# Constants loaded in three parts instead of one, with the first order table laid anew

## The chip, the cores and the metric

The kernel runs on one core of a Trainium2 chip. The metric is the device time of one execution in microseconds (us), as the median of the runs. The core has a matrix engine (TensorE, PE in the profile, with its weight loads as PEld), a vector engine (DVE), a scalar engine (ACT), GpSimd (POOL) and SyncE (SP), which here only issues loads and stores.

## What is computed

The reference is an attention-like retention layer without softmax, followed by a gated layer that mixes along the sequence:

```python
B, H, S, D = 8, 8, 576, 64
scores = (q @ k.T) / sqrt(D)                       # per batch and head
ret    = scores * where(rel >= 0, gamma[h] ** rel, 0)
x      = (ret @ v)                                 # -> (B, 576, 512)
h      = relu(x @ w_in)                            # (B, 576, 1024)
u, v   = h[..., :512], h[..., 512:]
v_n    = (v - mean(v)) / sqrt(var(v) + 1e-6)
v_s    = einsum('ts,bsd->btd', w_spatial, v_n) + b_spatial[None, :, None]
out    = (u * v_s) @ w_out
```

## The kernel before

The retention is computed in chunks of 128 rows (four per batch, and a tail of 64). A chunk `c` of batch `b` goes through these steps, and the order tables name each by a letter:

- `d.b.c`: its loads: `qk` (q and k, 512 KB), `kn` (k by rows, 256 KB), `vv` (v, 256 KB); chunks 2 and 3 of batch 0 come as one load of 1024 KB into the room of `u` and of `lent_wout`.
- `g.b.c`: PE makes the scores (`r<-qk`), then DVE multiplies them with the decay mask (`at<-r,fixed_terms`).
- `k.b.c`: `kn` is multiplied with powers of gamma. `q.b.c`: q is multiplied with powers of gamma into `qsc`.
- `p.b.c`: PE makes the update of the state (`r<-vv,kn`), then the state is taken on: `sh` (after half the chunk), `dec`, `st`.
- `b.b.c`: PE adds what the state carries (`r<-qsc,sh` and `r<-qsc,st`) in two halves, with a two-element copy on ACT between them (`r<-warm`), then the values (`r<-at,vv`); the result is split into a rounded part and the rest (`slot`, on ACT, then DVE).

The gated layer follows as large matrix products. `w.kind.i` turns a quarter of a weight matrix, which comes as float64 words, into a rounded part and the rest: one step on DVE or POOL, one on ACT, two on DVE, one on ACT (`win<-lent_vn`), one on POOL or DVE. `D.kind.i` loads such a quarter (512 KB), `c.a` loads the constants, `c.t` a mask for the tails. `z.i.1` is one product of 512 columns on a tile of zeros (`m<-wsp`), whose result nobody reads; there are 43 of them. I call them idle products.

The order of all work is written out in tables of such names: `ORDER` for batches 0 and 1 and the beginning of 2, then `STEADY` once for each batch, then `LAST`. Each name, when its turn comes, runs the chain's next step, and each engine keeps the order in which its instructions were written. `BANKS` says which of four result banks of `m` each large product takes.

The constants are one array, with 780 numbers (3120 bytes) for each of 128 rows, 390 KB in all, and one load:

```python
fixed_terms = cp.tile([P, 2 * NP * D + NP * D + H + NP], F32, name="fixed_terms")
am = fixed_terms[:, :512]...       # the decay mask, used by g (DVE)
qs = fixed_terms[:, 512:768]...    # powers for q, used by q (POOL, DVE)
kd = fixed_terms[:, 768:768 + H]   # powers for k, used by k
sd = fixed_terms[:, 768 + H:]      # powers for the state, used by p
```

SP issues loads in the order of the table. Each load counts on one of eight semaphores in turn, so the ninth waits until the first has landed, and so on.

Of the kernel before, what the change touches and what calls it, by code (L numbers as in the profile page):

```python
# [18 lines left out]
P = 128  # L19
# [29 lines left out]
    w.1.2.pp b.0.1 p.0.1.aa w.1.2.pp b.0.1 b.0.1 z.20.1 v.0.0 z.27.1 z.17.1 z.39.1 z.22.1 w.1.1.vp b.0.1 p.0.1.aa
    b.0.1 v.0.1 w.1.2.pp w.1.2.pp k.0.2.a g.0.2 p.0.2.aa w.1.2.pp w.1.1.vp w.1.3.vp w.1.2.pp v.0.0 z.42.1 v.0.1  # L50
    z.36.1 v.0.0 v.0.0 v.0.1 v.0.1 D.0.2 D.0.1 d.0.3 w.0.2.pp q.0.2.p p.0.1.aa w.0.2.pp p.0.2.aa g.0.2 p.0.2.aa
    p.0.2.aa w.0.2.pp w.0.1.vp w.0.1.vp w.0.1.vp w.0.2.pp w.0.1.vp T.0 S d.1.0 S d.1.0 d.1.0 c.t D.0.0 S d.1.1
    d.1.1 d.1.1 t.0.p q.0.3.p k.1.0.p k.0.3.a b.0.2 g.0.3 b.0.2 v.0.0 t.0.p b.0.2 b.0.2 p.0.3.ap p.0.2.aa b.0.2
    v.0.0 b.0.2 p.0.3.ap v.0.1 v.0.0 v.0.0 t.0.p g.0.3 v.0.1 z.26.1 z.29.1 z.11.1 z.5.1 v.0.2 v.0.2 v.0.2 z.9.1
    v.0.2 z.23.1 z.24.1 z.14.1 v.0.0 p.0.3.ap p.0.3.ap w.0.0.vp b.0.3 s.2.p v.0.1 b.0.3 g.1.0 v.0.0 w.0.0.vp v.0.2
    g.1.0 w.0.0.vp b.0.3 b.0.3 p.1.0.pp g.1.1 e.0.v e.0.v e.0.v w.0.0.vp v.0.1 v.0.4 v.0.4 v.0.4 z.16.1 z.35.1
    s.1.p b.0.3 w.0.2.pp p.1.0.pp w.0.0.vp v.0.1 b.0.3 v.0.3 v.0.3 v.0.4 v.0.3 v.0.3 q.1.0.p s.2.p k.1.1.p s.1.p
    p.1.0.pp w.0.0.vp d.1.2 S S v.0.2 w.0.1.vp v.0.2 v.0.2 s.3.p v.0.2 v.0.4 v.0.1 v.0.2 U.0 U.1 b.1.0 v.0.4 s.5.p
    v.0.4 v.0.3 s.0.p p.1.0.pp v.0.4 p.1.1.pp v.0.4 b.1.0 U.1 v.0.3 U.0 v.0.3 s.4.p g.1.1 v.0.3 v.0.3 v.0.4 v.0.3
    v.0.4 b.1.0 b.1.0 D.2.1 d.1.2 T.1 D.2.0 D.2.2 d.1.2 s.3.p w.0.2.pp q.1.1.p d.1.3 d.1.3 d.1.3 D.0.3 s.0.p G.1.2  # L60
    q.1.2.p p.1.0.pp s.5.p s.4.p v.0.4 v.0.4 p.1.1.pp p.1.1.pp p.1.1.pp w.0.1.vp k.1.2.p p.1.1.pp w.0.3.pv V.0.0
    V.0.0 V.0.0 V.0.0 V.0.3 V.0.0 V.1.0 b.1.0 V.0.0 b.1.0 V.0.3 w.2.1.vp w.2.1.vp V.1.0 w.2.1.vp V.1.2 V.0.2
    w.2.1.vp w.2.0.vv V.1.2 w.2.0.vv b.1.1 p.1.2.pa w.2.1.vp b.1.1 w.0.3.pv w.2.0.vv G.1.2 w.2.0.vv w.0.3.pv
    w.0.3.pv g.1.2 b.1.1 b.1.1 w.0.3.pv V.0.2 V.1.1 G.0.2 v.1.0 D.2.3 d.2.0 d.2.0 A.0.5.v A.0.0.v w.0.3.pv g.1.2
    p.1.2.pa w.2.2.vv G.0.3 V.1.1 w.2.0.vv p.1.2.pa p.1.2.pa G.0.2 q.1.3.p A.0.1.p k.1.3.p w.2.2.vv G.0.3 A.0.2.v
    A.0.6.v t.1.p V.0.1 G.0.1 p.1.2.pa V.0.1 b.1.1 b.1.1 w.2.0.vv v.1.0 A.0.9.v A.0.12.v w.2.2.vv p.1.3.pp b.1.2
    b.1.2 A.0.3 A.0.7 A.0.13.v A.0.14 P.0.1.p w.2.2.vv G.0.1 g.1.3 t.1.p b.1.2 b.1.2 v.1.0 V.1.3 v.1.0 G.1.3 v.1.1
    v.1.1 v.1.1 v.1.1 A.0.15.v p.1.3.pp w.2.3.vp p.1.3.pp w.2.1.vp d.2.1 d.2.0 d.2.1 b.1.2 t.1.p g.1.3 b.1.2 V.1.3
    A.1.5.p v.1.0 w.2.3.vp G.1.3 w.2.3.vp w.2.3.vp p.1.3.pp k.2.0.v v.1.0 b.1.3 b.1.3 p.2.0.vp b.1.3 g.2.0 b.1.3
    G.1.1 e.1.v P.0.0.p v.1.0 e.1.v e.1.v v.1.0 G.1.1 P.0.0.p P.0.1.p v.1.4 v.1.4 v.1.4 y.1.2.0 v.1.4 p.2.0.vp  # L70
    v.1.1 v.1.1 w.2.3.vp v.1.0 v.1.1 v.1.0 b.1.3 w.2.2.vv y.1.2.0 v.1.4 A.0.10 P.1.0.v y.1.1.0 y.1.1.0 A.0.4.v
    A.1.1.v w.2.2.vv v.1.1 v.1.1 v.1.1 g.2.0 p.2.0.vp y.1.0.0 F.0.0.0 y.1.0.0 F.0.0.0 P.1.1.v A.0.11.v A.0.8.v
    P.1.1.v b.1.3 v.1.4 F.0.0.2 v.1.2 v.1.2 F.0.0.1 v.1.2 v.1.2 v.1.4 w.2.3.vp F.0.0.1 F.0.0.2 v.1.2 A.1.0.v
    p.2.0.vp p.2.0.vp A.1.2.p A.1.3 P.1.0.v F.0.1.0 F.0.0.0 F.0.0.1 A.1.6.v A.1.9.v v.1.2 A.1.12.p v.1.4 A.1.13.v
    A.1.7 F.0.1.0 F.0.1.1 v.1.2 F.0.1.1 F.0.0.3 F.0.0.3 v.1.4 v.1.4 v.1.4 v.1.4 v.1.2 v.1.4 q.2.0.v F.0.0.3 F.0.1.0
    F.0.1.1 F.0.0.2 F.0.1.3 F.0.1.3 A.1.14 v.1.3 v.1.3 v.1.3 v.1.3 F.0.1.2 g.2.1 b.2.0 v.1.3 v.1.3 v.1.3 F.0.1.2
    v.1.3 b.2.0 v.1.3 y.1.3.1 y.1.2.1 y.1.3.1 k.2.1.a y.1.2.1 y.1.1.1 A.2.1.v A.1.4.p A.2.5.v A.1.15.p A.2.0.p
    A.2.2.v A.2.6.v v.1.3 A.2.9.v A.1.8.v A.2.12.v y.1.1.1 A.2.7 v.1.2 b.2.0 b.2.0 T.2 d.2.1 p.2.1.vv d.2.2 d.2.2
    d.2.2 F.0.1.3 y.1.3.0 g.2.1 v.1.2 X.1.1.2 X.1.1.2 A.2.3 A.2.10 A.1.10 b.2.0 X.1.0.0 X.1.0.1 y.1.0.1 q.2.1.v
    t.2.v A.2.11.v p.2.1.vv y.1.3.0 A.2.8.v b.2.1 b.2.1 p.2.1.vv p.2.1.vv k.2.2.v p.2.1.vv A.1.11.v X.1.0.1 X.1.0.0  # L80
    A.2.13.v A.2.14 y.1.0.1 A.2.15.v g.2.2 b.2.1 p.2.2.vv b.2.1 d.2.3 d.2.3 d.2.3 X.1.1.3 X.1.1.0 X.1.1.1 g.2.2
    A.2.4.v p.2.2.vv X.1.1.3 p.2.2.vv p.2.2.vv X.1.1.0 b.2.1 Y.1.3.p Y.1.1.v k.2.3.v Y.1.1.v X.1.1.1 Z.1.5.vv
    X.1.0.2 q.2.2.p b.2.2 b.2.2 Y.1.3.p Z.1.7.vv p.2.2.vv X.1.0.2 Z.1.6.vv p.2.3.vp t.2.v b.2.2 g.2.3 b.2.2
# [967 lines left out]
```

## Time and profile before

| | |
|---|---|
| time, median of 3 runs (lowest to highest) | 503.83 us (503.58 to 503.89) |
| profiled execution, its own time | 504.22 us |
| its span, from first to last instruction | 502.4 us |
| PE busy | 495.2 us, 99% of the span |
| DVE, ACT, POOL busy | 391.3, 259.4, 154.1 us |

The profiled execution took 1.8 us more than its span, which is launch and end around it. It is 0.39 us above the median. Busy time is the time in which an engine had an instruction running; the ends of matrix products are modelled, so a wait of PE that is shorter than about the length of a product can hide in it. Times in the rows count from the start of the span.

### The profile page before, as it was taken

What the parts mean: (1) busy time and instruction counts of PE and PEld (TensorE: products, weight loads), DVE (VectorE), ACT (ScalarE), POOL (GpSimd) and SP (SyncE); (2) the same over time, 40 slices, a digit from 0 to 9 for tenths busy, and PEclk for the clock granted to TensorE, in tenths of its full rate; (3) what the DMA queues carried; (4) which work ended last, traced back from release to release, by engine and by line L of the source; (5) the groups of instructions that cost most, each with busy time, mean ns of one, the idle gap of its engine ahead of it and who ended that gap; (6) DMA issues with size and microseconds to landing.
All of it is one profiled execution on the core that took longest, in us unless ns stands there. A gap on an engine that the chain in (4) does not pass through costs nothing.

```text
span 502.4 us, 17010 instructions
## 1 busy us (share of the span) xinstructions
PE 495.2 (99%) x7335; PEld 472.8 (94%) x7335; DVE 391.3 (78%) x869; ACT 259.4 (52%) x587; POOL 154.1 (31%) x133
## 2 busy tenths in 40 slices
...
DMA packets 26429, 55.53 MB, mean 111 GB/s; under 512 B 2929, under 2 KB 11249, under 8 KB 26098
## 3 DMA queue, kind: packets, MB, share of 16 engines
...
q14 instruction: 18, 0.15, 0.1%
...
## 4 chain that ended last, share of the span: by engine, by line
PE 94%; DVE 2%; ACT 1%; DMA 1%; issue 1%; POOL 0%; SPq 0%; ACTq 0%
PE m L203 79%; PE r L203 14%; DMA vv<-in_qkv 1%; ACT places L203 0%; DVE x L203 0%; POOL x L203 0%; DVE u L203 0%; DVE lent_vn L203 0%; DVE m L203 0%; ACT slot L203 0%; SPq L203 0%; DVE o L203 0%; DVE xt L203 0%; ACT xt L203 0%; DVE places L203 0%
## 5 line engine op out<-in xcount | busy, mean ns | idle before, releaser
L203 PE MATMUL m<-wsp,vn 128*128 128x288 f32 x768 | 112.7, 296 | 0.0
L203 PEld LDWEIGHTS m<-wsp,vn 128*128 128x128 f32 x768 | 105.0, 188 | 0.6
L203 DVE TENSOR_TENSOR u<-m,u 128x288 f32<-128x288 f32 (+1 forms) x132 | 57.1, 438 | 23.2 <-PE m L203 11.9
L203 ACT COPY u<-m 128x288 f32<-128x288 f32 (+1 forms) x92 | 34.8, 386 | 40.8 <-PE m L203 33.4
L203 PE MATMUL m<-slot,win 128*128 128x288 f32 x336 | 49.8, 296 | 0.0
L203 PEld LDWEIGHTS m<-slot,win 128*128 128x128 f32 x336 | 46.3, 188 | 0.9 <-ACT vn L203 0.2
L203 ACT CAST slot<-u 128x576 fp32r<-128x576 f32 x32 | 21.5, 675 | 45.3 <-DVE u L203 44.6
L203 DVE SCALAR_TENSOR_TENSOR u<-u,m 128x288 f32<-128x288 f32 x48 | 21.3, 451 | 26.6 <-PE m L203 26.4
L203 PE MATMUL m<-slot,wout 128*128 128x288 f32 x264 | 37.5, 294 | 0.0
L203 PEld LDWEIGHTS m<-slot,wout 128*128 128x128 f32 x264 | 36.0, 188 | 0.2
L203 PE MATMUL m<-win,slot 128*128 128x512 f32 (+1 forms) x168 | 36.2, 349 | 0.0
L203 ACT CAST places<-u 128x576 fp32r<-128x576 f32 x21 | 14.2, 675 | 39.0 <-DVE u L203 39.0
L203 POOL TENSOR_TENSOR dec<-st,fixed_terms 128x256 f32<-128x256 f32 x16 | 14.3, 895 | 64.6 <-DVE st L203 64.6
L203 POOL TENSOR_TENSOR qk<-qk,fixed_terms 128x512 f32<-128x512 f32 (+1 forms) x16 | 21.9, 1369 | 35.3 <-PE r L203 29.9
L203 PEld LDWEIGHTS m<-win,slot 128*128 128x128 f32 x168 | 26.7, 188 | 4.2 <-DVE slot L203 0.5
L203 PE MATMUL m<-quarter,slot 128*128 128x256 f32 x216 | 28.9, 281 | 0.1
L203 POOL TENSOR_TENSOR slot<-u,slot 128x576 fp32r<-128x576 f32 x7 | 10.0, 1436 | 59.5 <-ACT slot L203 53.9
L203 PEld LDWEIGHTS m<-quarter,slot 128*128 128x128 f32 x216 | 27.1, 188 | 0.7 <-ACT u L203 0.3
L203 PE MATMUL m<-wtl,vt 128*128 128x288 f32 (+1 forms) x128 | 27.2, 295 | 0.0
L203 PE MATMUL m<-places,wout 128*128 128x288 f32 x168 | 26.3, 297 | 0.0
L203 PE MATMUL m<-slot,part 128*128 128x288 f32 x168 | 25.3, 298 | 0.0
L203 DVE TENSOR_TENSOR at<-r,fixed_terms 128x512 f32<-128x512 f32 x32 | 21.9, 683 | 3.9 <-PE r L203 2.0
...
## 6 DMA issues: line engine op xcount, KB each, us to landing
qk<-in_qkv SPq DMA_DIRECT2D x30, 512.0 KB, 4.0
kn<-in_qkv SPq DMA_DIRECT2D x30, 256.0 KB, 4.6
vv<-in_qkv SPq DMA_DIRECT2D x30, 256.0 KB, 4.3
...
lent_slot<-in_w_v SPq DMA_DIRECT2D x4, 512.0 KB, 8.4
raw<-in_w_u SPq DMA_DIRECT2D x4, 512.0 KB, 10.8
```

What stands on the lines that cost most here:

```text
L203: ins = op(*args, **kw)
```

## The change

The array of constants becomes three, each with its own tile and load: `steps` (powers for k and for the state, 12 numbers a row, 6 KB in all) into `fixed_steps`, `terms` (the mask, 512 numbers a row, 256 KB) into `fixed_terms`, and `qterms` (powers for q, 256 numbers a row, 128 KB) into `qs`. In the tables `c.k`, `c.a` and `c.q` load them. `ORDER` and `BANKS` are new; `STEADY` and `LAST` stay. Every engine has the same instructions as before, in kind, number and shape, in another order; two loads are added on SP. The number of idle products stays at 43.

```diff
-    d.0.0 m z.41.1 z.34.1 d.0.0 c.a d.0.0 k.0.0.v q.0.0.p z.33.1 z.37.1 z.1.1 z.12.1 z.18.1 z.25.1 z.15.1 z.10.1
+    d.0.0 z.37.1 z.38.1 c.k d.0.0 m z.25.1 z.22.1 z.8.1 z.41.1 z.14.1 z.39.1 z.3.1 k.0.0.v d.0.0 g.0.0 c.q D.1.0
+    c.a q.0.0.p D.1.3 d.0.1 d.0.1 d.0.1 p.0.0.va p.0.0.va z.32.1 z.10.1 z.17.1 w.1.0.vp z.1.1 z.13.1 z.12.1 b.0.0
...
-    fixed_terms = cp.tile([P, 2 * NP * D + NP * D + H + NP], F32, name="fixed_terms")
-    am = fixed_terms[:, :512].rearrange("r (i p n) -> r i p n", i=2, p=NP)
-    qs = fixed_terms[:, 512:768].rearrange("r (p n) -> r p n", p=NP)
-    kd = fixed_terms[:, 768:768 + H].rearrange("r (h n) -> r h n", n=1)
-    sd = fixed_terms[:, 768 + H:].rearrange("r (p n) -> r p n", n=1)
+    fixed_terms = cp.tile([P, 2 * NP * D], F32, name="fixed_terms")
+    am = fixed_terms.rearrange("r (i p n) -> r i p n", i=2, p=NP)
+    fixed_steps = cp.tile([P, H + NP], F32, name="fixed_steps")
+    kd = fixed_steps[:, :H].rearrange("r (h n) -> r h n", n=1)
+    sd = fixed_steps[:, H:].rearrange("r (p n) -> r p n", n=1)
+    qs = cp.tile([P, NP, D], F32, name="qs")
...
-        "c": lambda k: dma_one(*{"a": (fixed_terms, terms), "t": (amt, tmask)}[k]),
+        "c": lambda k: dma_one(*{"a": (fixed_terms, terms), "k": (fixed_steps, steps), "q": (qs, qterms), "t": (amt, tmask)}[k]),
...
-    terms = np.concatenate([a.reshape(P, -1) for a in (am, qscale, kdec, per ** D)], axis=1)
-    return {"terms": f(terms), "tmask": f(amt)}
+    steps = np.concatenate([kdec, per ** D], axis=1)
+    return {"steps": f(steps), "terms": f(am.reshape(P, -1)), "qterms": f(qscale), "tmask": f(amt)}
```

On SP, the first loads of the program were these (`lent_slot<-in_w_v` are quarters of the weights; a number behind a name is that of a buffer, and x2 stands for two rows that read alike):

```order
L203 DMA qk_94<-in_qkv 128x1024
L203 DMA kn_95<-in_qkv 128x512
L203 DMA fixed_terms<-in_terms 128x780
L203 DMA vv_96<-in_qkv 128x512
L203 DMA lent_slot_93<-in_w_v 128x512 x2
L203 DMA qk_196<-in_qkv 128x1024
L203 DMA kn_197<-in_qkv 128x512
L203 DMA vv_198<-in_qkv 128x512
L203 DMA lent_slot_93<-in_w_v 128x512 x2
L203 DMA u<-in_qkv 128x2048
```

and are now these:

```order
L204 DMA qk_96<-in_qkv 128x1024
L204 DMA fixed_steps<-in_steps 128x12
L204 DMA kn_97<-in_qkv 128x512
L204 DMA vv_98<-in_qkv 128x512
L204 DMA qs<-in_qterms 128x256
L204 DMA lent_slot_95<-in_w_v 128x512
L204 DMA fixed_terms<-in_terms 128x512
L204 DMA lent_slot_95<-in_w_v 128x512
L204 DMA qk_137<-in_qkv 128x1024
L204 DMA kn_138<-in_qkv 128x512
L204 DMA vv_139<-in_qkv 128x512
L204 DMA lent_slot_95<-in_w_v 128x512 x2
```

The 6 KB for k come ahead of `kn`; the mask moves from third place to seventh, behind a quarter of the weights. `u`, the chunk 2 of batch 0, is the last row before, and follows right behind the last row now. The loads ahead of the second weight quarter are the same bytes in both, and so are those ahead of all that follows it down to `u`.

On PE, where chunk 0 of batch 0 begins (the first row is the last of 13 idle products; an instruction of 64x64 here is two in the trace):

```order
L203 MATMUL m_86<-wsp_68 128x512
L203 MATMUL r_91<-qk_94 64x64 x16
L203 MATMUL r_91<-vv_96,kn_95 64x64 x16
L203 MATMUL m_87<-wsp_68 128x512
L203 MATMUL m_88<-wsp_68 128x512
L203 MATMUL r_90<-qsc_106,sh 64x64 x4
L203 MATMUL m_89<-wsp_68 128x512
L203 MATMUL r_90<-qsc_106,sh 64x64 x4
L203 MATMUL r_90<-at_161,vv_96 64x64 x16
```

and now (the first row is the last of 9 idle products):

```order
L204 MATMUL m_88<-wsp_70 128x512
L204 MATMUL r_93<-qk_96 64x64 x16
L204 MATMUL r_93<-vv_98,kn_97 64x64 x16
L204 MATMUL m_89<-wsp_70 128x512
L204 MATMUL m_90<-wsp_70 128x512
L204 MATMUL m_91<-wsp_70 128x512
L204 MATMUL m_88<-wsp_70 128x512
L204 MATMUL m_89<-wsp_70 128x512
L204 MATMUL m_90<-wsp_70 128x512
L204 MATMUL r_92<-qsc_134,sh 64x64 x8
```

Four idle products fewer stand ahead of the first scores, and more of them between the update and what the state carries. Five idle products follow here, then the values, one idle product and chunk 1's scores. Counted over the whole order, 23 idle products stood ahead of chunk 1's update (`r<-vv,kn`) and 21 do now; ahead of its values 26 and 25; ahead of chunk 2's scores (`r<-u`) 31 and 29.

On ACT, around the small copy that stands between the two halves of what the state carries into chunk 1 (the last row but one; `m<-lent_slot` begins a weight quarter, `win<-lent_vn` rounds one):

```order
L203 ACTIVATE dec_78<-st_76,fixed_terms 128x64 x4
L203 CAST win_66<-lent_vn_92 128x512 x2
L203 ACTIVATE m_87<-lent_slot_93 128x512
L203 COPY r_90<-warm 1x2
L203 ACTIVATE dec_79<-sh,fixed_terms 128x64 x4
```

and now:

```order
L204 ACTIVATE dec_80<-st_78,fixed_steps 128x64 x4
L204 CAST slot_215<-r_92 128x2x4x64
L204 CAST win_68<-lent_vn_94 128x512
L204 ACTIVATE m_88<-lent_slot_95 128x512
L204 CAST win_68<-lent_vn_94 128x512
L204 COPY r_92<-warm 1x2
L204 ACTIVATE dec_81<-sh,fixed_steps 128x64 x4
```

The third weight quarter (`m<-lent_slot`) stands between the two roundings now, ahead of the second of them and of the copy.

## Rows read from the trace of the kernel before

**Rows 1.** The page: busy time of PE, and the chain that ended last, by engine.

```profile
PE 495.2 (99%) x7335; PEld 472.8 (94%) x7335; DVE 391.3 (78%) x869; ACT 259.4 (52%) x587; POOL 154.1 (31%) x133
PE 94%; DVE 2%; ACT 1%; DMA 1%; issue 1%; POOL 0%; SPq 0%; ACTq 0%
```

**Rows 2.** Busy time by stretch: PE, PEld, DVE, ACT, POOL, clock, DMA share, GB/s.

```profile
0.00:18.00 18.00, 15.21 (x269) 11.37 (x270) 9.50 (x20) 8.20 (x21) 6.92 (x11) 1.00 0.89 338
10.00:12.00 2.00, 2.00 (x45) 1.64 (x45) 1.53 (x5) 0.83 (x2) 0.00 (x0) 1.00 1.05 412
18.00:150.00 132.00, 131.94 (x2128) 122.50 (x2127) 107.64 (x221) 80.54 (x195) 58.37 (x50) 1.00 0.42 144
150.00:175.00 25.00, 24.60 (x421) 23.48 (x421) 20.91 (x52) 12.86 (x29) 14.82 (x12) 1.00 0.54 174
```

**Rows 3.** Timeline of the start: start, duration, instruction, idle before and its releaser.

```profile
1.50 5.58 PE L203 MATMUL m<-wsp 128*128 128x512 f32 x13 [1.50 <-DVE wsp L203]
...
6.79 0.69 DVE L203 TENSOR_TENSOR kn<-kn,fixed_terms 128x512 f32<-128x512 f32 x1 [5.34 <-DMA fixed_terms<-in_terms]
...
8.05 0.69 PE L203 MATMUL r<-vv,kn 64*64 64x64 f32 x32 [0.33 <-DMA vv<-in_qkv]
```

**Rows 4.** Timeline of SP: when loads were issued.

```profile
1.16 0.42 SPq L203 DMA_DIRECT2D kn<-in_qkv  x1
1.63 0.42 SPq L203 DMA_DIRECT2D fixed_terms<-in_terms  x1
2.09 0.43 SPq L203 DMA_DIRECT2D vv<-in_qkv  x1
2.57 0.91 SPq L203 DMA_DIRECT2D lent_slot<-in_w_v  x2
...
5.60 1.44 SPq L203 DMA_DIRECT2D lent_slot<-in_w_v  x2
7.93 0.33 SPq L203 DMA_DIRECT2D u<-in_qkv  x1
```

**Rows 5.** DMA view of each of those issues: KB, us from issue to landing.

```profile
kn<-in_qkv SPq DMA_DIRECT2D x1, 256.0 KB, 3.9
fixed_terms<-in_terms SPq DMA_DIRECT2D x1, 390.0 KB, 5.1
vv<-in_qkv SPq DMA_DIRECT2D x1, 256.0 KB, 5.8
lent_slot<-in_w_v SPq DMA_DIRECT2D x1, 512.0 KB, 6.6
lent_slot<-in_w_v SPq DMA_DIRECT2D x1, 512.0 KB, 9.5
u<-in_qkv SPq DMA_DIRECT2D x1, 1024.0 KB, 10.9
```

**Rows 6.** Timeline of chunk 1, from the seven idle products ahead of it.

```profile
10.99 1.88 PE L203 MATMUL m<-wsp 128*128 128x512 f32 x7
...
11.79 0.69 DVE L203 TENSOR_TENSOR slot<-r,slot 128x512 fp32r<-128x512 f32 x1 [0.43 <-ACT slot L203]
...
12.36 1.04 POOL L203 TENSOR_TENSOR kn<-kn,fixed_terms 128x512 f32<-128x512 f32 x1 [4.29 <-DMA kn<-in_qkv]
...
13.46 0.69 PE L203 MATMUL r<-vv,kn 64*64 64x64 f32 x32
...
15.70 0.64 ACT L203 ACTIVATE m<-lent_slot 128x512 f32<-128x512 f32 x1
...
16.27 0.14 ACT L203 COPY r<-warm 1x2 f32<-1x2 f32 x1
```

**Rows 7.** Timeline of chunk 2: scaling on ACT, scores on PE, then twelve weight loads.

```profile
18.87 2.02 ACT L203 ACTIVATE u<-u,fixed_terms 128x64 f32<-128x64 f32 x8
...
20.17 1.16 PE L203 MATMUL r<-u 64*64 64x64 f32 x64
...
23.00 2.75 PEld L203 LDWEIGHTS m<-win,slot 128*128 128x128 f32 x12
```

More of the change, by code (lines that the diff above doesn't have):

```diff
@@ L49 @@
[L49 to L83, printed above, removed]
@@ new lines @@
+    b.0.0 w.1.0.vp b.0.0 g.0.0 p.0.0.va p.0.0.va w.1.3.vp w.1.3.vp p.0.0.va z.4.1 z.31.1 z.15.1 z.24.1 z.29.1 b.0.0
+    z.19.1 k.0.1.p q.0.1.p w.1.3.vp w.1.3.vp w.1.0.vp b.0.0 g.0.1 w.1.3.vp b.0.0 w.1.0.vp p.0.1.aa z.26.1 z.16.1
+    p.0.1.aa D.1.1 D.1.2 w.1.1.vp g.0.1 w.1.1.vp w.1.0.vp d.0.2 w.1.0.vp w.1.2.pp b.0.1 z.34.1 z.7.1 b.0.1 b.0.1
+    b.0.1 p.0.1.aa w.1.2.pp b.0.1 v.0.0 z.2.1 z.9.1 z.28.1 w.1.1.vp w.1.1.vp w.1.1.vp b.0.1 v.0.1 z.5.1 w.1.2.pp
+    p.0.1.aa w.1.2.pp k.0.2.a g.0.2 p.0.2.aa w.1.1.vp w.1.2.pp w.1.2.pp w.1.3.vp q.0.2.p p.0.1.aa p.0.2.aa g.0.2
@@ new lines @@
+    p.0.2.aa v.0.0 z.11.1 z.6.1 v.0.1 v.0.0 v.0.1 v.0.1 z.20.1 D.0.1 d.0.3 D.0.2 T.0 w.0.1.vp w.0.1.vp w.0.1.vp
+    p.0.2.aa w.0.1.vp k.0.3.a D.0.0 S d.1.0 d.1.0 D.2.1 w.0.2.pp c.t S d.1.1 d.1.0 d.1.1 S d.1.1 t.0.p k.1.0.p
+    q.0.3.p b.0.2 b.0.2 v.0.1 w.0.2.pp w.0.1.vp p.0.2.aa g.0.3 t.0.p b.0.2 z.40.1 z.36.1 v.0.0 v.0.1 w.0.2.pp
+    w.0.2.pp p.0.3.ap b.0.2 p.0.3.ap g.0.3 z.0.1 z.27.1 z.35.1 z.21.1 z.18.1 b.0.2 b.0.2 v.0.2 z.42.1 v.0.0 z.33.1
+    v.0.1 v.0.2 p.0.3.ap v.0.2 z.30.1 v.0.2 v.0.1 t.0.p v.0.0 v.0.0 p.0.3.ap v.0.0 w.0.0.vp w.0.0.vp w.0.0.vp
@@ new lines @@
+    w.0.2.pp b.0.3 b.0.3 v.0.0 s.1.p g.1.0 g.1.0 b.0.3 b.0.3 g.1.1 p.1.0.pp v.0.0 e.0.v v.0.1 e.0.v w.0.0.vp v.0.4
+    v.0.4 z.23.1 v.0.4 v.0.4 q.1.0.p w.0.2.pp b.0.3 v.0.2 v.0.1 b.0.3 v.0.3 v.0.3 v.0.3 v.0.3 d.1.2 S k.1.1.p s.1.p
+    s.0.p w.0.0.vp p.1.0.pp p.1.0.pp v.0.4 w.0.0.vp s.0.p w.0.1.vp v.0.2 e.0.v v.0.2 v.0.2 s.3.p v.0.2 v.0.3 S
+    s.4.p s.2.p g.1.1 v.0.2 v.0.4 U.0 U.1 v.0.4 v.0.3 p.1.0.pp v.0.3 U.0 v.0.3 b.1.0 b.1.0 p.1.1.pp b.1.0 b.1.0
+    s.3.p s.2.p s.5.p p.1.0.pp s.5.p d.1.2 D.2.0 D.0.3 d.1.2 D.2.2 v.0.4 v.0.3 v.0.3 U.1 v.0.4 v.0.4 w.2.1.vp
@@ new lines @@
+    p.1.1.pp s.4.p V.0.0 V.0.0 V.0.0 V.0.0 G.1.2 p.1.1.pp k.1.2.p v.0.4 b.1.0 q.1.1.p w.0.3.pv v.0.4 v.0.4 V.1.2
+    V.1.2 G.1.2 V.1.0 V.0.0 w.2.1.vp w.2.1.vp w.2.1.vp V.1.0 b.1.0 p.1.1.pp G.0.2 V.0.2 V.0.2 G.0.2 V.0.0 g.1.2
+    b.1.1 p.1.2.pa w.0.3.pv b.1.1 b.1.1 b.1.1 w.0.3.pv w.0.3.pv w.2.0.vv V.1.3 w.0.3.pv w.0.3.pv b.1.1 w.2.2.vv
+    p.1.1.pp p.1.2.pa p.1.2.pa q.1.2.p V.1.3 w.2.0.vv g.1.2 w.2.0.vv b.1.1 w.2.0.vv A.0.0.v A.0.1.p A.0.2.v
+    p.1.2.pa A.0.5.v d.1.3 d.1.3 q.1.3.p V.0.3 v.1.0 G.0.3 v.1.0 V.0.3 T.1 t.1.p k.1.3.p v.1.0 v.1.0 V.0.1 V.1.1
@@ new lines @@
+    v.1.0 G.0.3 A.0.6.v p.1.2.pa V.0.1 w.2.0.vv V.1.1 v.1.1 v.1.1 b.1.2 D.2.3 d.1.3 d.2.0 d.2.0 k.2.0.v w.2.2.vv
+    A.0.7 b.1.2 A.0.3 A.0.9.v w.2.0.vv A.0.12.v v.1.0 v.1.0 A.0.13.v g.1.3 t.1.p p.1.3.pp b.1.2 b.1.2 G.0.1 b.1.2
+    p.1.3.pp p.1.3.pp b.1.2 G.0.1 p.1.3.pp v.1.1 v.1.1 G.1.3 g.1.3 v.1.0 t.1.p A.0.4.v d.2.0 b.1.3 g.2.0 p.2.0.vp
+    P.0.1.p G.1.3 w.2.2.vv v.1.1 v.1.1 w.2.2.vv A.0.10 w.2.1.vp w.2.1.vp P.0.0.p A.0.14 b.1.3 w.2.2.vv b.1.3 b.1.3
+    e.1.v v.1.1 G.1.1 e.1.v G.1.1 e.1.v v.1.0 P.1.1.v q.2.0.v P.0.0.p P.0.1.p F.0.0.1 y.1.2.0 F.0.0.1 P.1.0.v
@@ new lines @@
+    y.1.2.0 P.1.0.v A.0.8.v A.1.1.v v.1.0 P.1.1.v v.1.1 v.1.1 v.1.4 v.1.4 v.1.4 v.1.4 y.1.3.0 y.1.3.0 F.0.0.1
+    F.0.1.1 v.1.4 F.0.1.1 F.0.0.0 v.1.2 v.1.2 v.1.2 v.1.2 v.1.4 v.1.4 A.0.15.v v.1.1 w.2.3.vp w.2.3.vp F.0.0.0
+    w.2.3.vp w.2.3.vp w.2.3.vp w.2.2.vv b.1.3 p.2.0.vp v.1.2 v.1.4 A.0.11.v p.2.0.vp F.0.1.0 d.2.1 d.2.1 F.0.0.0
+    d.2.1 F.0.1.0 A.1.5.p F.0.0.2 F.0.0.2 y.1.1.0 v.1.4 y.1.1.0 w.2.3.vp F.0.0.3 A.1.0.v A.1.2.p v.1.4 b.1.3 v.1.4
+    v.1.4 F.0.0.3 y.1.2.1 y.1.2.1 A.1.3 v.1.3 v.1.3 v.1.3 v.1.3 g.2.0 v.1.2 v.1.2 v.1.2 A.1.9.v p.2.0.vp v.1.4
@@ new lines @@
+    v.1.3 v.1.3 A.1.6.v F.0.1.3 F.0.1.2 k.2.1.a F.0.0.3 F.0.1.3 v.1.2 p.2.0.vp A.2.0.p A.1.4.p A.1.12.p A.2.1.v
+    v.1.2 b.2.0 F.0.0.2 F.0.1.1 p.2.1.vv b.2.0 b.2.0 b.2.0 g.2.1 F.0.1.2 v.1.3 v.1.3 v.1.3 F.0.1.3 y.1.0.0 y.1.3.1
+    y.1.0.1 d.2.2 d.2.2 T.2 F.0.1.0 d.2.2 A.2.2.v g.2.1 v.1.3 A.1.7 y.1.0.0 y.1.0.1 A.1.13.v p.2.1.vv A.1.14
+    A.2.5.v A.2.9.v q.2.1.v A.2.6.v p.2.1.vv A.2.7 p.2.1.vv X.1.0.1 X.1.0.0 y.1.1.1 A.1.15.p A.1.8.v b.2.0 b.2.1
+    b.2.1 A.2.10 A.1.10 A.2.8.v p.2.1.vv X.1.0.1 A.2.12.v k.2.2.v g.2.2 y.1.1.1 A.2.3 p.2.2.vv b.2.1 b.2.1 y.1.3.1
```

27 lines of the change are left out of this document (13 added, 14 removed).

## The prediction

> **What bounds the kernel now.** I read the page first. PE is busy for 99% of the span, and the chain that ended last runs through PE for 94% [rows 1]. Every engine has the same instructions after the change, so PE's work cannot shrink: only the time in which PE waits, or runs slowly, can change. Busy time by stretch says how much of that there is. PE lacks 18.00 - 15.21 = 2.79 us in the first 18 us, 0.06 us from there to 150 us, and 0.40 us between 150 and 175 us [rows 2]. Of the 2.79 us, 1.50 pass before the first product [rows 3], which the change leaves alone. The other 1.29 us, with 0.06 and 0.40, make 1.75 us that a new first table could save at the very most by waits. A measurement of this kernel can tell about 0.2%, 1.0 us, from no change; more than half of those waits would have to go.
>
> PE is slow at the start too: 13 idle products take 5.58 us there, 0.43 us each, and the same product takes at most 1.88 / 7 = 0.27 us later [rows 3, 6]. 512 columns in 0.43 us is the clock's level of 1.2 GHz, in 0.21 us that of 2.4 GHz; PE had done nothing before these products, and nothing but them until the clock rose (the column of the granted clock reads 1.00 for the whole stretch all the same [rows 2]). In a dense stretch twelve weight loads take 2.75 us, 0.23 us for each product of 512 columns [rows 7]. I price an idle product at 0.23 us.
>
> Next the timeline, for what PE and its feeders wait for at the start. The first `kn` multiplication on DVE waits until 6.79 us for the constants. PE makes chunk 0's update at 8.05 us, when `vv` has landed [rows 3]. Issue plus time to landing gives 1.16 + 3.9 = 5.1 us for `kn`, 1.63 + 5.1 = 6.7 for the constants, 2.09 + 5.8 = 7.9 for `vv`, 2.57 + 6.6 = 9.2 for the first weight quarter, 5.60 + 9.5 = 15.1 for the third, and 7.93 + 10.9 = 18.8 for `u` [rows 4, 5]. They land one behind the other, and the DMA engines are full: share 1.05 and 412 GB/s from 10 to 12 us [rows 2]. So the start is paced by bytes. The planned order gives PE idle products while it waits for them.
>
> **The change, step by step.** Everything is counted from the profiled execution, as a difference, and put on the median of 503.83 us (the profiled execution itself took 504.22, 0.39 above).
>
> *The early start.* `kn`'s multiplication now needs 6 KB and `kn` alone. At the earliest `kn` lands at 5.1 us as before, at the latest 0.66 later (what the extra load can cost is worked out below). With 0.69 us for the multiplication that is 5.8 to 6.5 us. `vv` now follows `kn` at once; its 256 KB take 0.64 us at 412 GB/s, and took 7.9 - 6.7 = 1.2 us. So it lands between 5.1 + 0.64 = 5.7 and 5.8 + 1.2 = 7.0 us, and the update of chunk 0 starts at 5.9 to 7.0 us, 1.0 to 2.1 us earlier than 8.05. PE is free for it: with 9 idle products ahead in place of 13 it is done with them about 4 x 0.43 = 1.7 us earlier.
>
> *What this meets.* The bytes ahead of the second weight quarter, and of all of chunk 1's loads and `u`, are the same as before, so the stream delivers these no earlier. It may deliver them later, by two more loads. At 412 GB/s the 390 KB (399 kB decimal) of constants are worth 0.97 us, and they took 6.7 - 5.1 = 1.6: up to 0.66 us over. The weight quarter, which is the first of its array too, took 9.2 - 7.9 = 1.3 us for 1.27: nothing over, and I use 0.0 as the lower end. Two loads cost 0 to 1.3 us. I take 0.2 each, 0.4 together: their own bytes are moved anyway, and in size they are nearest to the loads that cost little.
>
> *Chunk 1.* Its `kn` was waited for by POOL until 12.36 us, was multiplied in 1.04 us, and PE's update followed at 13.46 us [rows 6]. It cannot come earlier now. By then PE had run 23 idle products, and will have run 21. Two have moved behind the gate: 2 x 0.23 = 0.46 us of PE work more is left when it opens, and the time that the early start won is spent waiting for `kn`. On ACT the small copy between the halves came at 16.27 us. Now the third weight quarter stands ahead of a rounding and of the copy: landing at 15.1, then 0.64 us [rows 6], then another rounding of about that size give 16.4 us, later by 0.1 and by the delay of the stream. Two idle products lie in that wait now, so I count nothing for it.
>
> *Chunk 2.* `u` landed at 18.8, and ACT began its eight scalings at 18.87 us; the scores on PE start at 20.17 us and end with the last scaling [rows 7]. This gate moves with the stream alone. PE has run 29 idle products there in place of 31. So at this gate PE is behind by 0.46 + 0.4 = 0.86 us.
>
> *What is won back behind it.* Waits of PE itself are no source: 0.06 us up to 150 us [rows 2]. DVE is: it is busy for 82% of that stretch (107.64 of 132), and its idle 0.43 us ahead of `slot` [rows 6] is filled in the new order, where two steps of a weight quarter stand ahead of `slot`. DVE's work may come 0 to 0.43 us earlier by that. I take it whole, since the idle products that moved behind the gate then stand where PE would have waited for DVE. BANKS only renames the banks; its cover is that the same four banks take as many products, and I count nothing. Issue time of two more loads on SP, 0.43 us each [rows 4], lies under a stream that is full: nothing.
>
> The sum: +0.46 + 0.4 - 0.43 = +0.43 us. 503.83 + 0.43 = 504.3 us, which is no difference that can be measured. Its own range runs from 0.46 + 0 - 0.43 = 0.0 (503.8) to 0.46 + 0.54 = +1.0 us (504.8).
>
> **The rivals.**
> *The stream catches up (faster).* Between 5.1 and 7.9 us, the constants and `vv` took 0.66 and 1.2 - 0.64 = 0.56 us over the stream's rate. If that hung on the one load with rows of 3120 bytes, it goes with it, and all that is gated by the stream opens 1.2 us earlier: +0.46 - 1.2 - 0.43 = -1.2 us, 502.6 us. For it speaks that the loss begins with that load; against it that `vv`, with another row length, is late too, which a lasting price of each new array would explain. Up to 175 us the 0.40 us of [rows 2] could go too.
> *Each load costs its full price (slower).* Both small loads cost 0.66 us and DVE's gap is not won: 0.46 + 1.3 = +1.8 us, 505.6 us. It decides once the stream is over 0.54 us late with nothing won back. For it speaks the row of the constants, against it the weight quarter.
> The Trainium skill, DMA: Bandwidth & Descriptors, section Rules for kernel authors, speaks against the change in this way: many small transfers should be coalesced, since under 64 KB one pays mostly overhead. By that page's fit of 2.0 us for each transfer (section Anatomy of one DMA, made for GpSimd's path), an estimate for two more in a row is 4.0 us, 507.8 us. The trace does not bear that out: each load took 3.9 us and more from issue to landing, yet they land 0.6 to 1.6 us apart.
> *A slow clock for longer (slower).* Fewer idle products run at the start, and PE waits for chunk 0's update. If the clock stays at 1.2 GHz until chunk 0's values, 11 idle products take 0.43 in place of 0.23 us: 2.2 us, of which the wait for chunk 1 hides 0.46 + 0.4. That is +1.3 more than forecast, 505.6 us. For it speaks that PE's start is lighter, against it that the first nine products still run back to back from 1.50 us.
>
> **How the numbers follow.** The forecast has 0.55, the stream that catches up 0.20, full price 0.15, the slow clock 0.10. The range of 8 in 10 goes from the faster rival, 502.6 us, to 505.5 us, just short of the two slow ones, of which it cuts off about half, as of the faster one's far side. Faster by over 0.2% is the first rival, 0.20; slower the other two, 0.25; the rest is 0.55.
>
> **What would show it.** Right: chunk 0's update on PE at 6 to 7 us, chunk 1's not before 13.4, with PE waiting just ahead of it, the scalings of `u` at 18.9 to 19.4 us, and 0 to 1 us more of PE's idle time in the first 18 us. Wrong: `u` landing well before 18.8 us (the first rival), or after 19.5 (full price); idle products of 0.43 us after chunk 0's update (the clock); or new waits of PE between 18 and 150 us, which I have priced at nothing because the order alone does not show them: a chain there that comes just too late would cost on top.

## The result, and the profile after

The changed kernel takes 506.90 us, median of 4 runs (506.43 to 507.05), and the kernel before 503.86 beside it: 1.0060 times as long, 95% interval 1.0042 to 1.0077, or 3.04 us slower. Measured once more (`e8_after_again`), the ratio was 1.0077 (1.0064 to 1.0090). The forecast was 504.3 us with a range to 505.5; the time lies above it. In some executions with the new order or the three loads TensorE's mean granted clock is 0.99, and these are 1 to 4 us longer (last section); of the executions whose profile stands here only that of `e2_three_loads` is one.

The changed kernel's profiled execution took 507.05 us, with a span of 505.3. Its page, busy time and the chain that ended last:

```profile
PE 496.2 (98%) x7335; PEld 472.9 (94%) x7335; DVE 395.6 (78%) x869; ACT 259.3 (51%) x587; POOL 155.1 (31%) x133
PE 84%; DVE 7%; DMA 4%; POOL 2%; ACT 2%; issue 1%; SPq 0%; ACTq 0%; DVEq 0%
```

PE is busy for 1.0 us more than before, and the chain leaves PE for 16% of the span instead of 6% [rows 1]. Busy time by stretch, columns as in [rows 2], says where:

```profile
0.00:18.00 18.00, 15.52 (x269) 11.22 (x270) 9.30 (x19) 8.56 (x22) 6.31 (x11) 1.00 0.91 339
18.00:150.00 132.00, 130.51 (x2113) 120.61 (x2112) 108.19 (x219) 78.28 (x191) 58.39 (x49) 1.00 0.42 144
150.00:175.00 25.00, 25.00 (x426) 24.01 (x425) 22.69 (x49) 13.50 (x30) 15.09 (x13) 1.00 0.51 167
```

PE is idle for 2.48 us in the first 18, where it was 2.79: they lost nothing by waits. PE waited 0.06 us between 18 and 150 us before, and waits 1.49 us there now. The start itself did what was foretold. Its timeline, with chunks 0 and 1, the copy and the scaling of `u` [rows 3, 6, 7]:

```profile
1.50 4.21 PE L204 MATMUL m<-wsp 128*128 128x512 f32 x9 [1.50 <-DVE wsp L204]
...
5.91 0.69 DVE L204 TENSOR_TENSOR kn<-kn,fixed_steps 128x512 f32<-128x512 f32 x1 [4.46 <-DMA kn<-in_qkv]
...
6.66 0.69 PE L204 MATMUL r<-vv,kn 64*64 64x64 f32 x32
7.28 1.66 PE L204 MATMUL m<-wsp 128*128 128x512 f32 x6
...
13.78 0.69 PE L204 MATMUL r<-vv,kn 64*64 64x64 f32 x32 [0.72 <-DMA vv<-in_qkv]
...
15.82 0.15 ACT L204 COPY r<-warm 1x2 f32<-1x2 f32 x1
...
18.43 2.02 ACT L204 ACTIVATE u<-u,fixed_steps 128x64 f32<-128x64 f32 x8
...
19.90 1.16 PE L204 MATMUL r<-u 64*64 64x64 f32 x64 [0.20 <-DVE st L204]
```

Chunk 0's update comes 1.4 us earlier (6.66 for 8.05), chunk 1's 0.3 us later, with PE waiting ahead of it, and the scaling of `u` 0.4 us earlier. Issues of loads on SP, and the DMA view's KB and us from issue to landing of four of them [rows 4, 5]:

```profile
2.09 0.43 SPq L204 DMA_DIRECT2D vv<-in_qkv  x1
2.57 0.43 SPq L204 DMA_DIRECT2D qs<-in_qterms  x1
...
5.84 0.48 SPq L204 DMA_DIRECT2D vv<-in_qkv  x1
...
8.43 0.33 SPq L204 DMA_DIRECT2D u<-in_qkv  x1
```

```profile
vv<-in_qkv SPq DMA_DIRECT2D x1, 256.0 KB, 4.4
qs<-in_qterms SPq DMA_DIRECT2D x1, 128.0 KB, 4.3
vv<-in_qkv SPq DMA_DIRECT2D x1, 256.0 KB, 7.8
u<-in_qkv SPq DMA_DIRECT2D x1, 1024.0 KB, 10.0
```

Chunk 0's `vv` lands at 2.09 + 4.4 = 6.5 us, the new load `qs` at 6.9, chunk 1's `vv` at 13.6 (before, issued at 5.11 and landed 7.9 later: 13.0), and `u` at 18.4 where it landed at 18.8. Most of the time was lost behind all that. The two largest new waits of PE are these:

```profile
53.39 0.54 PE L204 MATMUL m<-wtl,vt 128*128 128x288 f32 x2 [0.86 <-DVE vt L204]
...
126.29 0.69 PE L204 MATMUL r<-vv,kn 64*64 64x64 f32 x32 [0.35 <-DVE kn L204]
```

What the first one waits for stands on ACT, then DVE. In the changed kernel:

```profile
49.43 0.69 ACT L204 ACTIVATE vt<-m,sm 64x512 fp32r<-64x512 f32 x1 [0.66 <-DVE sm L204]
51.39 0.59 ACT L204 CAST slot<-r 128x512 fp32r<-128x512 f32 x1 [1.28 <-POOL wtl L204]
51.87 0.68 ACT L204 ACTIVATE vt<-m,sm 64x512 fp32r<-64x512 f32 x1
...
52.59 0.74 DVE L204 SCALAR_TENSOR_TENSOR vt<-m,sm,vt 64x512 fp32r<-64x512 f32 x1 [2.18 <-ACT vt L204]
```

And in the kernel before, the same rows of ACT and the first product that needs them:

```profile
48.55 1.26 ACT L203 ACTIVATE vt<-m,sm 64x512 fp32r<-64x512 f32 x2
51.44 0.59 ACT L203 CAST slot<-r 128x512 fp32r<-128x512 f32 x1 [1.64 <-POOL wtl L203]
...
51.65 0.70 PE L203 MATMUL m<-wtl,vt 128*128 128x288 f32 x4
```

`vt` is the normed tail of batch 0 that the first gated products need; the CAST writes batch 1's first values over room that POOL still reads for `wtl`, until 51.4 us in both kernels. Before, both `vt` instructions were through when ACT came to that wait. In the new order the second stands behind the CAST, and with it DVE's part and PE.

The second wait is DVE's. Its rows ahead of `kn`, and POOL's beside them:

```profile
120.54 0.69 DVE L204 TENSOR_TENSOR room<-room 128x512 f32<-128x512 f32 x1
121.14 1.52 DVE L204 TENSOR_TENSOR dec<-sh,fixed_steps 128x256 f32<-128x256 f32 x1
...
124.95 0.68 DVE L204 TENSOR_TENSOR room<-wout,wout 128x512 f32<-128x512 f32 x1
125.55 0.68 DVE L204 TENSOR_TENSOR kn<-kn,fixed_steps 128x512 f32<-128x512 f32 x1
126.15 1.78 DVE L204 TENSOR_TENSOR room<-room 128x512 f32<-128x512 f32 x1
...
120.82 1.56 POOL L204 TENSOR_TENSOR quarter<-x,quarter 128x512 fp32r<-128x512 f32 x1 [3.18 <-ACT quarter L204]
```

DVE works without a gap there, `kn` is simply the last of a row, and one instruction of 0.42 us took 1.52. Those 1.1 us are more than the wait; no run takes them away alone.

To follow PE over the whole span I use its lag: the durations that PE's products have where nothing delays them (0.231, 0.132, 0.117 and 0.016 us for 512, 288, 256 and 64 columns) are added up in PE's order, and two kernels are compared at the same sum. It is worked out from the matmul rows of each trace, against the run `e11_before_again`. The columns are times in that run, the last of them the start of its last product; us:

```
                         17.6   22.1   26.1   48.7   53.7  121.1  129.4  162.4  498.4
before (rows 1 to 7)    -0.01  -0.01   0.00  -0.34  -0.34  -0.34  -0.34  -0.34   0.34
changed                  0.01   0.18   0.27   0.37   1.51   1.25   1.76   1.74   2.68
e8_after_again           0.30   0.46   0.55   0.66   1.76   1.48   1.96   1.93   2.27
e1_vt_ahead              0.43   0.60   0.69   0.79   0.79   0.53   1.03   1.02   1.81
e5_kn_ahead             -0.23  -0.06   0.05   0.15   0.14  -0.11  -0.18   0.33   0.69
e3_one_load              0.63   0.50   0.65   0.76   1.87   1.60   2.08   2.07   2.55
e4_block_put_in         -0.06   0.33   0.34  -0.22   1.64   1.61   1.61   1.60   1.84
e14_new_last            -0.46  -0.46  -0.45  -1.04  -1.04  -1.07  -1.06  -0.99  -1.05
```

The step of 1.1 us between 48.7 and 53.7 us and that of 0.5 between 121.1 and 129.4 stand out. Up to 17.6 us two runs of one order differ by up to 0.7 us; that scatter is carried on, so steps are to be read, not levels. The two orders have done the same products at each of these times but 26.1 us. (The profiled run of before had a wait of 0.40 us at 170 us, put down to issue, which `e11_before_again` has not: chance. `e11_before_again` has one of its own, 0.26 us at 28.36, also put down to issue, which before, `e4_block_put_in` and `e14_new_last` have not.)

### The profile page after: what moved, and what is told of

Same layout as the page of the kernel before. It is cut to its first block, busy times and chain, and to the rows that moved or that the text cites. A ratio compares the mean times of both kernels' runs of the same rounds, so it can differ in the third digit from the quotient of the medians.

```text
span 505.3 us, 17013 instructions
## 1 busy us (share of the span) xinstructions
PE 496.2 (98%) x7335; PEld 472.9 (94%) x7335; DVE 395.6 (78%) x869; ACT 259.3 (51%) x587; POOL 155.1 (31%) x133
## 4 chain that ended last, share of the span: by engine, by line
PE 84%; DVE 7%; DMA 4%; POOL 2%; ACT 2%; issue 1%; SPq 0%; ACTq 0%; DVEq 0%
PE m L204 72%; PE r L204 12%; DMA lent_slot<-in_w_v 2%; DMA raw<-in_w_u 1%; DVE u L204 1%; DVE room L204 1%; DMA vv<-in_qkv 1%; DVE sm L204 1%; POOL wtl L204 1%; DVE vn L204 1%; POOL win L204 1%; DVE x L204 0%; DVE s L204 0%; DVE qk L204 0%; DVE dec L204 0%
## 5 line engine op out<-in xcount | busy, mean ns | idle before, releaser
L204 POOL TENSOR_TENSOR dec<-st,fixed_steps 128x256 f32<-128x256 f32 x16 | 13.7, 857 | 63.0 <-DVE st L204 60.3
L204 POOL TENSOR_TENSOR qk<-qk,qs 128x512 f32<-128x512 f32 (+1 forms) x16 | 21.5, 1343 | 28.2 <-PE r L204 23.5
L204 POOL TENSOR_TENSOR kn<-kn,fixed_steps 128x512 f32<-128x512 f32 x15 | 16.1, 1075 | 29.2 <-DMA kn<-in_qkv 29.2
```

The costliest lines, as they stand in the source:

```text
L204: ins = op(*args, **kw)
```

## The experiments

**The changed kernel again**, as the measure for the runs beside it: `e8_after_again`, no edit.

> The changed kernel once more, as the measure for the three beside it: 506.4 to 507.2 us, with TensorE's waits of 0.86 us at 53.4 and 0.35 to 0.55 us at 126.3 in the same places. If the wait at 126.3 is chance it will be absent here.

506.67 us, 1.0077 (1.0064 to 1.0090). The waits are there again, at 53.66 and 126.49 us.

**The block at 53 us, taken out and put in.** In the order of the changed kernel, `b.1.0` (its CAST into `slot`) goes behind the last two `v.0.4` (ACT's second `vt`, DVE's part):

```diff
- k.1.2.p v.0.4 b.1.0 q.1.1.p w.0.3.pv v.0.4 v.0.4
+ k.1.2.p v.0.4 q.1.1.p w.0.3.pv v.0.4 v.0.4 b.1.0
```

> The changed kernel with one row of ScalarE's moved: both vt instructions ahead of the slot CAST that waits for GpSimd's last wtl (51.4 us); nothing else. Theory A (the blocked row costs): TensorE's 0.86 us wait before m<-wtl,vt at 53.39 goes, TensorE is there at about 52.5, and the end comes 0.9 to 1.1 us earlier: 505.8 to 506.0 us. Rival B (the late row only uncovers a later wait that takes the time back, in 60 to 130 us): the wait at 53.39 goes, the time stays at 506.9. Rival C (the cause lies in the loads or in the first 50 us): nothing moves but 0.2.

506.34 us, 1.0059 (1.0043 to 1.0075); by time alone not told from the changed kernel. The profile tells: ACT's rows and PE's first product that needs them are now

```profile
49.85 1.26 ACT L204 ACTIVATE vt<-m,sm 64x512 fp32r<-64x512 f32 x2 [0.66 <-DVE sm L204]
51.81 0.59 ACT L204 CAST slot<-r 128x512 fp32r<-128x512 f32 x1 [0.70 <-POOL wtl L204]
...
52.79 0.43 PE L204 MATMUL m<-wtl,vt 128*128 128x288 f32 x2
```

with no wait of PE, and the lag has no step there (0.79 and 0.79); at 121 us it is 0.95 below that of the changed kernel again, though this run began 0.13 later. C falls. Of that gain 0.5 to 0.9 us is left at the last product (1.81 for 2.27 and 2.68), so B is not ruled out by this run alone. The kernel before with the same row moved the other way:

```diff
- s.5.p s.4.p v.0.4 v.0.4 p.1.1.pp
+ s.5.p s.4.p b.1.0 v.0.4 v.0.4 p.1.1.pp
...
- V.1.0 b.1.0 V.0.0 b.1.0
+ V.1.0 V.0.0 b.1.0
```

> The kernel before with one row of ScalarE's moved: the slot CAST that waits for GpSimd's wtl (51.4 us) ahead of the second vt instruction, as it stands in the changed kernel. Theory A: vt's second part comes at 51.9, VectorE's part at 52.6, TensorE's first m<-wtl,vt at 53.4 in place of 51.7 with a wait of 1.5 to 1.7 us, and the time is 505.3 to 505.6 if nothing takes it back, at least 504.9. Rival B (slack later in the program takes it back): 503.9 to 504.3.

505.60 us, 1.0037 (1.0025 to 1.0049): 1.9 us slower than the kernel before by one row.

```profile
51.54 0.59 ACT L203 CAST slot<-r 128x512 fp32r<-128x512 f32 x1 [2.18 <-POOL wtl L203]
52.02 0.68 ACT L203 ACTIVATE vt<-m,sm 64x512 fp32r<-64x512 f32 x1
...
53.54 0.81 PE L203 MATMUL m<-wtl,vt 128*128 128x288 f32 x4 [1.64 <-DVE vt L203]
```

The lag rises by 1.86 us there, to 1.64, and is 1.84 at the end: nothing gives it back. So Theory A holds here by time as well, and B falls. Of the two kernels the changed one loses less by it (1.1), because its PE comes to that product 0.9 us later (53.39 - 0.86 = 52.5 for 51.65).

**Loads or order.** The order of before with three loads:

```diff
- d.0.0 c.a d.0.0 k.0.0.v
+ c.k d.0.0 d.0.0 c.q c.a k.0.0.v
```

> The kernel before with its own table of order and of banks, but its constants in three loads: the powers of k at the place of the one load, ahead of kn; the powers of q and the mask right behind vv. Theory A (the table costs, not the loads): 503.5 to 504.2 us, at most 0.4 from the kernel before; the first update comes about 1 us earlier, which the second chunk's loads take back. Rival B (two more loads delay the stream at their full price of 1.3 to 1.8 us): 505.2 to 505.7. Rival C (the earlier start is kept): 502.7 to 503.

504.07 us, 1.0014 (0.9999 to 1.0029). In its profiled execution `u` was issued at 7.84 us and landed 11.6 later, at 19.4:

```profile
u<-in_qkv SPq DMA_DIRECT2D x1, 1024.0 KB, 11.6
```

And the new order with one load:

```diff
- d.0.0 z.37.1 z.38.1 c.k d.0.0 m
+ d.0.0 z.37.1 z.38.1 d.0.0 c.a m
...
- g.0.0 c.q D.1.0 c.a q.0.0.p
+ g.0.0 D.1.0 q.0.0.p
```

> The changed kernel's tables of order and banks, with the constants in one load again, behind kn as in the kernel before. Theory A (the table costs): 506.5 to 507.3 us, and the waits at 53.4 and 126.3 us stand there as in the changed kernel; the first update comes at about 8 us again, at no cost or 0.3. Rival B (the loads cost): 503.9 to 504.5. Rival C (both, about half each): 505.3.

507.26 us, 1.0087 (1.0062 to 1.0111). Its first update stands at 7.93 us again, and both waits at 53.77 and 126.62 us. So the order costs, the loads hardly; and the 1.3 us by which the three loads bring the first update forward are worth nothing that shows behind it (lag at 22.1 us: 0.50 with one load, -0.06 to 0.60 with three).

**The wait at 126 us.** On top of `e1_vt_ahead`, `kn` one row ahead on DVE:

```diff
- X.1.0.1 A.2.12.v k.2.2.v g.2.2
+ X.1.0.1 k.2.2.v A.2.12.v g.2.2
```

> The changed kernel with both vt instructions ahead of the slot CAST and, besides, one row of VectorE's moved: the scaling of kn that TensorE waits for at 126 us stands ahead of room<-wout,wout, the 0.68 us row before it. Theory A: the wait of 0.35 before r<-vv,kn goes (kn ends at 125.3 to 125.7 in place of 126.2, ahead of TensorE's 125.9), and the time is 0.4 to 0.55 below the same kernel without this move: 505.3 to 505.7, or 1.4 to 1.6 below the changed kernel. Rival B: the room rows put behind it are late in their turn, or the wait returns at the next VectorE row that TensorE needs: no more than 1.1 below the changed kernel.

505.89 us (505.04 to 508.44), 1.0065 (1.0046 to 1.0084). The wait is gone, and the long `room` behind it delays nobody:

```profile
123.57 0.68 DVE L204 TENSOR_TENSOR kn<-kn,fixed_steps 128x512 f32<-128x512 f32 x1
124.17 0.68 DVE L204 TENSOR_TENSOR room<-wout,wout 128x512 f32<-128x512 f32 x1
124.89 1.66 DVE L204 TENSOR_TENSOR room<-room 128x512 f32<-128x512 f32 x1
...
124.40 0.65 PE L204 MATMUL r<-vv,kn 64*64 64x64 f32 x32
```

The lag has no step there (-0.11 and -0.18 for 1.48 and 1.96). The span is 503.3 us, 1.6 below that of the changed kernel again, as Theory A has it; the medians alone (0.8 lower) would not settle it.

**Idle products behind 18 us.** 18 left out of `e5_kn_ahead`, 16 out of the kernel before; they multiply zeros and nobody reads them:

```diff
-        spin(name, n)
+        spin(name, 0 if int(name[4:]) in LEFT_OUT else n)
```

> As the run with kn moved ahead, and with the 18 idle products left out that TensorE works off behind 17.9 us (they multiply zeros and nobody reads them). Theory A (from 18 to 40 us TensorE waits for nobody, and the 0.45 to 0.65 us lost there are idle products that stand where TensorE has real work): up to 18 x 0.231 = 4.2 us fall away, 501 to 503 us. Rival B (other engines' chains set the pace there and the idle products lie in their waits): waits of the same length take their place, 505.2 to 505.8. Rival C (TensorE's granted clock falls where they are gone): a stretch at the lower clock in the profile, and 507 or more.

505.40 us, 1.0045 (1.0033 to 1.0057). Between 18 and 40 us PE is idle for 2.8 us in place of 0.3:

```profile
18.00:40.00 22.00, 19.20 (x444) 14.23 (x444) 17.42 (x38) 19.41 (x57) 15.32 (x13) 1.00 0.94 346
```

Rival B: the other engines set the pace there, and the products lie in their waits.

> The kernel before with the 16 idle products left out that TensorE works off behind 18.3 us. Theory A (they stand in TensorE's own time): up to 16 x 0.231 = 3.7 us fall away, 500 to 502 us. Rival B (they lie in waits for other engines): 503.4 to 504.0. Rival C (the granted clock falls): 506 or more.

504.09 us, 1.0015 (1.0007 to 1.0024), nearest to Rival B; a little slower, so they don't cost in the kernel before either. The granted clock stayed at 1.00 in both.

**Where the rest lies.** First two halves, joined at 38.6 us of PE (behind `v.0.4 v.0.4 v.0.4` of either order):

```
e9:  before's order up to  z.16.1 z.35.1   then the changed order's remaining rows, both waits mended
e10: changed order up to   z.23.1 v.0.4 v.0.4   then before's remaining rows
```

> The kernel before up to 38.6 us of TensorE (its constants in one load, its order and banks), and from there the order and banks of the changed kernel with both mends (vt ahead of the slot CAST, kn ahead of room; bank numbers 0 and 2 exchanged so that the halves fit). Theory A (what is left after the two mends, 1.2 to 2 us over the kernel before, lies in the first 40 us): 503.3 to 503.9 us, within 0.1 per cent of the kernel before. Rival B (it lies behind 40 us, in the many small waits up to the end): 504.7 to 505.5. Half each would be 504.3.

505.41 us, 1.0037 (1.0025 to 1.0050).

> The other half: the changed kernel up to 38.6 us of TensorE (three loads, its order and banks), and from there the order and banks of the kernel before (bank numbers 0 and 2 exchanged). Theory A: 0.8 to 1.5 us over the kernel before, 504.3 to 505.0, with neither of the waits at 53 and 126 us. Rival B: 503.3 to 503.9, since the first 40 us cost nothing. If the granted clock falls in the first 20 us in some executions, as in the profiled one of the three loads in the old order, those are 3 us longer.

509.76 us (507.25 to 512.08), 1.0125 (1.0096 to 1.0153). Neither answers the question: at the joint `e9` waits for `slot` at 39.22 and 40.13 us and `e10` for POOL at 43.2 and 44.5, 1 us and more that neither kernel has.

The kernel before again:

> The kernel before once more, to see which of its profile's waits are chance: if the 0.4 to 0.6 us wait that its profile has at 170 us is absent, that profile was 0.7 us longer than a common one, and the sum of what the changed kernel lost is to be made against 0.7 us less; 503.2 to 503.9 us.

503.34 us, 0.9996 (0.9987 to 1.0006), span 502.1; the wait at 170 us is absent.

Then thirds, joined where both orders have done nearly the same rows:

```
e12: changed order up to  d.0.3 D.0.2                  then before's remaining rows
e13: before's up to  g.0.2 p.0.2.aa, changed (both waits mended) up to  Z.1.5.vv, then before's
e14: before's up to  X.1.1.1 Z.1.5.vv                  then the changed order's remaining rows
```

> The changed kernel's first 25 us (three loads, its order and banks), then the kernel before's order and banks to the end; cut where the two orders have done nearly the same work (3 rows of the table apart), so that no seam should cost. Two mended waits explain 1.6 of the 2.8 to 3.3 us; of the 1.2 to 2 us left, Theory A (the start: chunk 1's powers come later in the stream, TensorE is 0.4 to 0.5 us late at 17.5 us on average, and 0.4 more by 40 us) gives 504.2 to 504.9 here. Rival B (the middle, 25 to 128 us) and C (the end, behind 128 us) give 503.2 to 503.7.

506.20 us, 1.0061 (1.0048 to 1.0075). The lag is 0.57 at 17.6 us, 0.75 at 26, and then a wait at the joint makes it 2.3:

```profile
28.94 0.46 PE L204 MATMUL r<-tail 64*64 64x64 f32 x16 [1.14 <-ACT r L204]
```

> The kernel before, with the order and banks of the changed kernel only between 25 and about 128 us, both waits mended there (vt ahead of the slot CAST, kn ahead of room). Theory A (start): 503.3 to 503.8. Rival B (middle): 504.4 to 505.2; the profile would then show TensorE falling behind between 25 and 128 us by about 1 us. Rival C (end): 503.2 to 503.7.

505.16 us, 1.0033 (1.0021 to 1.0045). The lag is 0.17 at 26 us and 0.24 at 129; 1.3 us of the rest come at once, at the second joint:

```profile
134.91 1.33 PE L203 MATMUL m<-wsp,vn 128*128 128x288 f32 x8 [1.09 <-DVE u L203]
```

> The kernel before up to about 128 us, then the order and banks of the changed kernel to the end. Theory A and Rival B: 503.2 to 503.8. Rival C (the bank numbers of the repeated stage and the order of the last rows of the table cost 0.5 to 1 us there): 504.0 to 504.6.

503.27 us, 1.0002 (0.9994 to 1.0011). What lies behind 128 us of the new order costs nothing by itself: Rival C falls. B does not: the middle of `e13_new_middle_mended` loses 0.1 us before its joint against `e11_before_again`, which has its own wait at 28.36 us, but 0.4 to 0.7 against the other three runs of the old order, and without the 1.3 us of the joint its time is still 0.5 above the kernel before. For Theory A speaks the lag at 22.1 us; the times of `e12_new_first_25` can't, by its joint.

## Why the prediction was wrong

*The early start* was right: chunk 0's update at 6.66 us, inside 5.9 to 7.0.

*What this meets* was right in kind: the stream stayed the gate, and two more loads cost little. By time `e2_three_loads` costs 0.14%, 0.7 us, with an interval from nothing to 1.5. At the full price of 1.3 us for the loads `e3_one_load`, which saves them, would have gained; it did not. So that rival falls, and so does the stream that catches up: no time came with the earlier `u`. The 0.4 us itself is not shown at `u`: it landed at 18.4 us in the changed kernel and at 19.4 in `e2_three_loads`, but in runs of the old order with one load too it landed anywhere from 18.2 (`e14`) to 19.2 (`e4`). Its scalings began at 18.43 and 20.31 us in those two, both outside the 18.9 to 19.4 us that I gave. The estimate of 4.0 us, made from the Trainium skill's page DMA: Bandwidth & Descriptors, section Anatomy of one DMA, is not borne out: the 128 KB of `qs` landed 0.4 us behind `vv`.

*Chunk 1* came at 13.78 us, after 13.46 as said, though for another load: its `vv`, not its `kn`. That `vv` landed at 13.3 to 13.9 us in the four runs that begin with the whole new front, three loads and new order (changed, `e8`, `e1`, `e5`), at 12.6 to 13.0 in four of the old one (before, `e11`, `e4`, `e14`), at 12.9 in `e3` and at 13.1 in `e2`: in these runs it is late with the loads and the order together, not with either alone. The copy on ACT came at 15.82 us instead of the 16.4 forecast. *The slow clock for longer* did not happen in the profiled run: nine idle products took 4.21 us, the six behind the update 1.66, 0.28 each.

*What is won back behind it.* The forecast was a lag of 0.43 us behind the start. At 22.1 us, behind chunk 2's scores, the same four runs of the new front lag by 0.30 us on average, the four of the old one by -0.03: 0.33 us, near the forecast and within the scatter. The terms behind that sum were others, so the fit is luck. In the kernel before PE waits for DVE's `sh` and for ACT here:

```profile
15.62 0.24 PE L203 MATMUL r<-qsc,sh 64*64 64x64 f32 x1 [0.57 <-DVE sh L203]
...
16.46 0.27 PE L203 MATMUL r<-qsc,st 64*64 64x64 f32 x1 [0.38 <-ACT r L203]
```

Both waits are gone in the new order, more than the 0.43 us that I counted. In their place stand 0.25 us for ACT at 9.57, 0.72 for `vv` at 13.78, and 0.20 for DVE's `st` ahead of chunk 2's scores, which I took to wait for `u` alone. Also, PE's idle time in the first 18 us fell by 0.31 us, where I expected 0 to 1 more.

At 48.7 us the two groups are 0.9 us apart (0.49 and -0.40). The 0.56 that came since 22.1 us lie behind the gates of the sum. A part may be this: by the matmul rows of before, each time that PE goes from products of 64 columns to longer ones and back, about 0.37 us pass beyond the products' own durations (an estimate, 0.24 and 0.13 as medians of some 40 such places), and the new order does so twice between 22 and 32 us, the old one once. From 49 to 121 us the new order does it once less, and all four new runs win 0.25 us back there. No run takes it alone, and the rest of the 0.56 is open.

*The step that failed* is the last one named: new waits between 18 and 150 us, "which I have priced at nothing because the order alone does not show them". One of 1.1 and one of 0.5 us came, shown by `e1`, `e4` and `e5`: 1.6 of the 3.04 us. The sentence that let them through was "Waits of PE itself are no source: 0.06 us up to 150 us". It holds for what can be won. For what can be lost it says the opposite: PE has no gap there, so what comes late on another engine reaches it at once, and little behind gives it back. And the first of them was to be had from the order and one row of before: ACT waits 1.64 us for POOL at 51.44, so whatever the new order puts behind that CAST is done after 52.0, and DVE's part of `vt` at about 53.3, for a product that PE wants at 51.65.

0.33 up to 22.1 us, 0.56 from there to 48.7, 1.1 at the first wait, -0.25 up to 121 and 0.5 at the second make 2.2 of 3.04 us (of 3.35 in `e8`). Behind 129 us the lag rises by 0.3 to 0.9 in the runs with the new order from start to end, by 0 to 0.7 in those with the old one, at many small places, and `e14_new_last` shows no cost of that part alone: some 0.4, within the scatter. The last 0.5 lies behind PE's last product, where no lag shows it. From SP's issue of the last store to the end of the span (502.4 and 505.3 us) it is 2.7 us in the kernel before and 3.2 in the changed one:

```profile
499.74 0.41 SPq L203 DMA_DIRECT2D out<-o  x1
```

```profile
502.08 0.40 SPq L204 DMA_DIRECT2D out<-o  x1
```

It is 2.7 us in `e11`, `e4` and `e14` too, 3.2 in `e8`, `e1` and `e5`, 3.0 in `e3` (new order, one load) and 2.9 in `e2` (old order, three loads). So the two loads cost 0.2 us at the end and the order 0.3; what the end waits for is open. None of the versions run beats the kernel before; `e14_new_last` equals it.
